# Weights first, two units' mixing shared with ScalarE, and filler transposes in a fused attention and channel-mix kernel

## The chip, the cores and the metric

The kernel runs on one core of a Trainium2 chip, in one launch. The metric is the device time in microseconds (us). A core has four compute engines that matter here: TensorE (PE in the profile: matmuls and transposes), VectorE (DVE), ScalarE (ACT) and GpSimd (POOL). SyncE (SP) issues every DMA. Each engine takes its instructions in the order of the program and waits at the first whose operands are not there.

## The reference

```python
# q, k, v: (8, 8, 576, 64); window 64
scores = q @ k.T / 8, kept where 0 <= i - j < 64
attn = exp(scores - rowmax);  attn /= attn.sum(-1) + 1e-9
x = (attn @ v), heads side by side: (8, 576, 512)
x_prev = x one row later, a zero row first
xk = mu_k * x + (1 - mu_k) * x_prev
xr = mu_r * x + (1 - mu_r) * x_prev
k = relu(xk @ w_k)            # 512 -> 1024
v = (k * k) @ w_v             # 1024 -> 512
out = sigmoid(xr @ w_r) * v
```

All tensors are float32; the three weight matrices come as 8-byte words (float64 bits) and are turned into float32 on the chip.

## The kernel before, in words

**Weights.** The weights are 20 chunks of 128 x 512 words (`chunks`, L169): four of w_r, eight of w_k, eight of w_v, 512 KB each. `load_w` (L173) issues a chunk's DMA, and `decode` (L191) turns it into two float32r parts: one ACT instruction (`sign`), four DVE instructions (`clamp`, `shift`, `top`, `low`: the profile's `wt`, `wp`, `wp`, `wt`), one ACT copy and one POOL subtraction (`ws`). Matmuls take an operand as two parts and make three products of them, so a "piece" of a product is three matmuls.

**Attention.** Blocks of 64 queries are taken in groups `t` of eight, for two heads at once. `burst` (L338) is one PE piece: the scores of group t (tile `s`, 32 small matmuls) and the values of group t-1 (tile `x`, 32). `soften` (L392) does the softmax: per 128 x 128 block a DVE reduction (`least`), an ACT exponential (`exp`), two small DVE instructions (`shares`, tile `rs`), a POOL scaling (`scale`), then four PE transposes into the single PSUM bank `t` (`flip`) and an ACT copy out of it (`keep`, tile `pt`). The result lands in `xT`, channels by tokens, in SBUF.

**Channel mix.** Tokens are taken in 11 units (`UNITS`, L25): 256 tokens, 320, then nine of 448. For each unit `mix` (L467) makes xr and xk in four chunks each: DVE `diff` (tile `d` = x - x_prev), DVE `blend` (d * mu + x_prev), ACT `high`, POOL `low`. `r_units`, `k_units` and `v_units` make the three products of a unit through `product` (L511); their PSUM banks are four of tag `m`, which the decoding also uses.

**Order.** Nothing is issued where it is written. Every step is a `Piece` with an engine, a key (its urgency; 40 keys to a unit, `USTEPS`), a cost in ns, what it needs and what buffers it takes. `play` (L96) runs a small simulation of the engines with those costs, always beginning the ready piece of lowest key, and the order in which pieces begin there is the program order of each engine. `LINK` (50) is the simulated delay from one engine to another. `BEGIN` (L43) has the keys of the groups, `DECODE` (L600) those of the chunks (from -28 to 22), and the transfers are issued in the order of L600 to L621: two pairs' first q and k columns, one chunk, two more pairs, one chunk, the first v columns, mu, three chunks, the rest of q and k, three chunks, the rest of v, the other twelve chunks.

Until the chunks are decoded, PE has only the first groups and unit 0 to work on. From then on its work is unit after unit, with a burst and two flips for every group in between.

Of the kernel before, what the change touches and what calls it, by code (L numbers as in the profile page):

```python
# [17 lines left out]
P = 128  # L18
# [23 lines left out]

BEGIN = (-30, -29, 0, 6, 12, 18, 26, 34, 43, *range(53, 184, 10),  # L43
         196, 210, 223, 236, 250, 263, 277, 286, 295, 304, 312, 322, 332, 342, 352)
LINK = 50

HI_MIN = struct.unpack("<f", struct.pack("<I", 0x38000000))[0]
HI_MAX = struct.unpack("<f", struct.pack("<I", 0x47EFFE00))[0]
# [3 lines left out]
def attn_rwkv_kernel(ctx, tc, qT, kT, v2, mu_k, mu_r, w_k, w_v, w_r, out):  # L52
# [43 lines left out]
    def play():  # L96

        left, free, now, begun = {}, {}, 0, []
        for n, p in enumerate(pieces):
            left.setdefault(p.engine, []).append((p.key, n, p))  # L100
            free[p.engine] = 0
        for e in left:
            left[e].sort(key=lambda x: x[:2])
        users = {id(h): len(h.users) for p in pieces for h in p.takes}
        ends = []
        times = [0]
        while any(left.values()):
            assert times, [(e, [(p.key, p.fn.__name__) for _, _, p in ps[:4]]) for e, ps in left.items()]
            now = heapq.heappop(times)
            while ends and ends[0][0] <= now:  # L110
                _, _, p = heapq.heappop(ends)
                for hold in (*p.takes, *p.uses):
                    users[id(hold)] -= 1
                    if not users[id(hold)]:
                        room[hold.tag] += 1
            for e, ps in left.items():
                if free[e] > now:
                    continue
                for i, (_, n, p) in enumerate(ps):
                    if not all(q.done is not None and q.done + (q.lag if q.engine != e else 0) <= now  # L120
                               for q in p.needs):
                        continue
                    tags = [h.tag for h in p.takes]
                    if any(room[tag] < tags.count(tag) + p.spare for tag in set(tags)):
                        continue
                    del ps[i]
                    for tag in tags:
                        room[tag] -= 1
                    free[e] = now + p.cost
                    p.done = free[e]  # L130
                    begun.append(p)
                    for at in (p.done, p.done + p.lag):
                        heapq.heappush(times, at)
                    heapq.heappush(ends, (p.done + p.lag, n, p))
                    break
        return begun

    def over(n):

# [22 lines left out]

    muk = const.tile([P, NC], F32, name="muk")
    mur = const.tile([P, NC], F32, name="mur")

# [23 lines left out]
    def decode(n, loaded):  # L191
        ws, _, i, c = chunks[n]
        key = DECODE[n]
        word, bits = Hold("tmp"), Hold("m")

        def sign():
            words[n] = tmp.tile([P, WC], F32, name="wt", tag="tmp", bufs=TB)
            sca.activation(words[n], raw[n][:, :, 1].bitcast(F32), AF.Abs)

        def clamp():  # L200
            dve.tensor_scalar(words[n], words[n], HI_MIN, HI_MAX, op0=ALU.max, op1=ALU.min)

        def shift():

            words[n, 0] = ps_m.tile([P, WC], U32, name="wp", tag="m")
            dve.tensor_scalar(words[n, 0], words[n].bitcast(U32), 3, 0x3FFFFFF8,
                              op0=ALU.logical_shift_left, op1=ALU.bitwise_and)

        def top():
            dve.scalar_tensor_tensor(words[n, 0], raw[n][:, :, 1], 0xC0000000, words[n, 0],  # L210
                                     op0=ALU.bitwise_and, op1=ALU.bitwise_or)

        def low():
            dve.scalar_tensor_tensor(words[n].bitcast(U32), raw[n][:, :, 0], 29, words[n, 0],
                                     op0=ALU.logical_shift_right, op1=ALU.bitwise_or)

        def first_part():
            ws[i, c] = const.tile([P, 2, WC], F32R, name="ws", tag="w", bufs=len(chunks))
            sca.copy(ws[i, c][:, 0], words[n])

        def second_part():
            pool.tensor_sub(ws[i, c][:, 1], words[n], ws[i, c][:, 0].bitcast(F32))

        p = Piece("ACT", key, 680, sign, [loaded], takes=[word])
        p = Piece("DVE", key, 420, clamp, [p])
        p = Piece("DVE", key, 700, shift, [p], takes=[bits])
        p = Piece("DVE", key, 700, top, [p])
        p = Piece("DVE", key, 690, low, [p], uses=[bits])
        p0 = Piece("ACT", key, 630, first_part, [p])
        decoded[id(ws), i, c] = p0, Piece("POOL", key, 1280, second_part, [p0], uses=[word])  # L230

# [105 lines left out]

    def burst(t, ts, tv):  # L338

        needs, takes, uses, cost = [], [], [], 200  # L340
        if ts is not None:
            for n, i in (half for halves in groups[ts] for half in halves):
                needs += [arrived[n, i], arrived[n, max(i - 1, 0)], arrived[n, min(max(i, 1), NB - 1)]]
                uses += held[n]
                cost += 54
            takes += [Hold("s"), Hold("s")]
        if tv is not None:
            for n, i, _, _ in order(tv):
                needs.append(arrived[(n, *chunk(i))])
                uses += held["v", n]  # L350
                cost += 61
            needs += chain.pop((tv, "kept"))
            uses += chain.pop((tv, "pt"))
            bank = Hold("x")
# [37 lines left out]
    def soften(t, h, p, bank):  # L392
# [1 line left out]
        key = BEGIN[t]  # L394
        count = len(groups[t])
        rows, sm = Hold("pr"), Hold("sums") if h == 0 else None
        exps = []
        for e in range(count):
            def least(e=e):
                if e == 0:  # L400
# [8 lines left out]
            def exp(e=e):  # L409
# [1 line left out]
                sca.activation(pr[:, e], pr[:, e], AF.Exp, bias=sums[t, h][0][:, e:e + 1], scale=-1.0,  # L411
                               accum_out=sums[t, h][1][:, e:e + 1])

            q = Piece("DVE", key + 0.5, 375, least, [p, exps and softened or None],
                      ([rows] if e == 0 else []), [bank])
            softened = q
            exps.append(Piece("ACT", key + 0.5, 590, exp, [q]))

        def shares():
            rs = sums[t, h][2][:, :count]  # L420
            dve.tensor_scalar_add(rs, sums[t, h][1][:, :count], EPS)
            dve.reciprocal(rs, rs)

        q = Piece("DVE", key + 0.5, 350, shares, exps)
        scaled = []
        for e in range(count):
            def scale(e=e):
                pr = weights[t, h]
                pool.tensor_scalar(pr[:, e], pr[:, e], sums[t, h][2][:, e:e + 1], 1.0, op0=ALU.mult, op1=ALU.mult)

            scaled.append(Piece("POOL", key + 0.5, 400, scale, [q]))

        def flip():
            ps = flipped[t, h] = ps_t.tile([P, G, P], F32, name="t")
# [29 lines left out]
            t += n  # L464
        return found

    def mix(u, mu, xs, hold, c, key):  # L467


        state, scratch = [], Hold("tmp")  # L470
# [1 line left out]
        for b, t0, n in parts(u):  # L472
            ns = b * NP + c

            def diff(o=o, n=n, ns=ns, t0=t0):
                if not xs:
                    xs.append(act.tile([P, 2, NC, TU], F32R, name=hold.tag))
                if o == 0:
                    state.append(tmp.tile([P, TU], F32, name="d", tag="tmp", bufs=TB))
                d = state[0]  # L480
                dve.tensor_sub(d[:, o:o + n], xTs[ns][:, 1 + t0:1 + t0 + n], xTs[ns][:, t0:t0 + n])

            def blend(o=o, n=n, ns=ns, t0=t0):
                d = state[0]
                dve.scalar_tensor_tensor(d[:, o:o + n], d[:, o:o + n], mu[:, c:c + 1], xTs[ns][:, t0:t0 + n],
                                         op0=ALU.mult, op1=ALU.add)

            needs = {got[ns, i] for i in range(max(t0 - 1, 0) // W, (t0 + n) // W)}
            takes = ([scratch] + ([hold] if c == 0 else [])) if o == 0 else []
            p = Piece("DVE", key, over(n), diff, [*needs, p, mixing.get(id(hold))], takes)  # L490
            mixing[id(hold)] = p
            p = Piece("DVE", key, over(n), blend, [p], uses=[held["x", ns]])
            o += n
# [5 lines left out]
            pool.tensor_sub(xs[0][:, 1, c, :o], state[0][:, :o], xs[0][:, 0, c, :o].bitcast(F32))  # L499

        p = Piece("ACT", key, over(o), high, [p])
        return p, Piece("POOL", key, 100 + 2.25 * o, low, [p], uses=[scratch])

    mixing = {}

    def weight(w, a, c, m):

        o = m * P
        return w[c, o // WC][:, a, o % WC:o % WC + P]

    def product(key, w, col, x, made, uses, count, n, spare=0):  # L511


        ps, bank, last = [], Hold("m"), None
        for c in range(count):
            def fn(c=c):
                if c == 0:
                    ps.append(ps_m.tile([P, 512], F32, name="m", tag="m")[:, :n])
                for a, e in ((0, 0), (0, 1), (1, 0)):
# [3 lines left out]
            needs = [last, *made[c], *decoded[id(w), c, col * P // WC]]  # L523
            last = Piece("PE", key + 3 * c / STEP, 3 * (13 + n / 2.4), fn, needs,
                         [bank] if c == 0 else [], uses(c), lag=200, spare=spare if c == 0 else 0)
        return ps, bank, last

    def r_units(key, xr, hold, made, gate, n):
# [23 lines left out]
    def k_units(key, xk, hold, made, k2, n):  # L552
        for f in range(NF):
# [17 lines left out]

            key += 3 * NC / STEP
            p = Piece("ACT", key, over(n), relu, [p], [scratch], [bank])
            p = Piece("POOL", key, 100 + 1.9 * n, square, [p])
            p0 = Piece("ACT", key, over(n), high, [p], [result])
            p1 = Piece("DVE", key, over(n), low, [p0], uses=[scratch])
            k2.append((state, result, (p0, p1)))
# [20 lines left out]


    DECODE = [-28 + 3 * n for n in range(4)] + [-10 + 2 * n for n in range(8)] + [8 + 2 * n for n in range(8)]  # L600
    for n in range(2):
        load_qk(n, 0, 4)
    load_w(1)
    for n in range(2, NP):
        load_qk(n, 0, 4)
    load_w(1)
    for n in range(NP):
        load_v(n, 0, 2, 0, 1)

    def vectors():  # L610
        dma.dma_start(muk, mu_k)
        dma.dma_start(mur, mu_r)

    arrived["mu"] = transfer(vectors, 4096)
    load_w(3)
    for n in range(NP):
        load_qk(n, 4, NB)
    load_w(3)
    for n in range(NP):
        load_v(n, 2, 4, 1, 4)  # L620
    load_w(len(chunks) - len(raw))  # L621
# [13 lines left out]
    for u, nb in enumerate(UNITS):  # L635
# [7 lines left out]
            keys = {"xr": (20, 22, 33, 35), "xk": (25, 27, 29, 31)}  # L643
        else:
            keys = {"xr": [base - 40 + k for k in (33, 35, 37, 39)], "xk": [base - 40 + k for k in (25, 27, 29, 31)]}
        for nm, mu in (("xr", mur), ("xk", muk)):
            hold = Hold(nm)
            xs[nm] = ([], hold, [])
            for c in range(NC):
                xs[nm][2].append(mix(u, mu, xs[nm][0], hold, c, keys[nm][c]))  # L650
        if u == 0:
            r_units(base, *xs["xr"], gate, n)
            k_units(base + 8, *xs["xk"], k2, n)
# [37 lines left out]
```

## Time and profile before

| | us |
|---|---|
| median of 3 runs (lowest, highest) | 689.8 (689.45, 691.6) |
| the profiled execution's own time | 691.39 |
| its span in the profile | 689.6 |
| PE busy in the span | 650.2 |
| DVE busy | 428.1 |
| ACT busy | 366.8 |
| POOL busy | 353.4 |

The span is what the profile covers of the execution; about 1.8 us of the device time lie around it. Busy times are unions of instruction times, and a busy PE need not run at its full clock: the granted clock stands beside it, 1.00 for full and 0.50 for half. In the tables by stretch, each row has the stretch, its length, then each engine's busy us with its count of instructions, the granted clock, the DMA engines' mean share and GB/s. In timelines a row has the start, the length, and the instruction group, with the idle time before it and who ended that in brackets.

### The profile page before, as it was taken

The page shows a single profiled execution, that of the slowest core. Times are in us where ns is not written, and L with a number is a line of the kernel's source. Part 1 is how long each engine was busy: PE and PEld are TensorE (multiplying, and loading weights), DVE is VectorE, ACT ScalarE, POOL GpSimd, SP SyncE. Part 2 cuts the span into 40 slices and gives each one's busy share as a digit, 9 for nine tenths or more (in the row PEclk, how much of TensorE's full clock was granted, in tenths as well). Part 3 has the DMA queues.
Part 4 walks back from the last instruction along what each step waited for, and adds up shares of the span by engine and source line. Part 5 has one row for each costly group of instructions (what it writes and reads, how often), then busy time and mean ns, then how long its engine had stood idle before and what let it go on. Part 6 is the DMA issues. An engine that isn't in the chain of part 4 may idle for free.

```text
span 689.6 us, 14350 instructions
## 1 busy us (share of the span) xinstructions
PE 650.2 (94%) x5232; PEld 583.5 (85%) x5232; DVE 428.1 (62%) x1372; ACT 366.8 (53%) x1111; POOL 353.4 (51%) x503
## 2 busy tenths in 40 slices
PE   5657888999999999999999999999999999999997
PEld 4446787998889888888889788988888889999997
DVE  2998985485487269447926824883595478177241
ACT  5547666656666475466446535736664563242430
POOL 4556776656666455446635543553555464244310
PEclk9756799999999999999999999999999999999999
DMA  8970232233223222322111232123212100001001
GB/s 254 300 316 0 71 127 97 66 114 122 66 67 106 79 66 80 106 82 95 54 52 36 80 106 66 66 66 120 66 46 75 66 2 27 28 1 40 14 1 54
DMA packets 33766, 56.50 MB, mean 82 GB/s; under 512 B 5024, under 2 KB 16800, under 8 KB 33696
## 3 DMA queue, kind: packets, MB, share of 16 engines
q1 hardware_dynamic: 33696, 55.59, 24.3%
q8 instruction: 41, 0.67, 0.4%
q14 instruction: 29, 0.24, 0.1%
HBM read 46.14 MB, written 9.44 MB: 81 GB/s over the span
## 4 chain that ended last, share of the span: by engine, by line
PE 81%; DVE 7%; POOL 4%; DMA 3%; issue 2%; ACT 2%; SPq 1%; POOLq 0%; ACTq 0%
PE m L73 68%; PE x L73 5%; PE s L73 4%; PE t L73 4%; POOL pr L73 2%; DVE wp L73 2%; DVE d L73 2%; DVE wt L73 2%; POOL ws L73 1%; DMA w<-w_k 1%; DMA k<-kT 1%; ACT pr L73 1%; SPq L73 1%; DMA v<-v 1%; DVE r L73 1%
## 5 line engine op out<-in xcount | busy, mean ns | idle before, releaser
L73 PE MATMUL m<-xk,ws 128*128 128x448 f32 (+2 forms) x1056 | 223.9, 365 | 5.1 <-ACT xk L73 1.8
L73 POOL TENSOR_SCALAR pr<-pr,rs 128x128 f32<-128x128 f32 x288 | 139.1, 500 | 146.8 <-DVE rs L73 124.4
L73 PE MATMUL m<-ks,ws 128*128 128x448 f32 (+2 forms) x1056 | 212.8, 357 | 0.0
L73 PEld LDWEIGHTS m<-xk,ws 128*128 128x128 f32 x1056 | 192.0, 195 | 21.1 <-POOL xk L73 2.2
L73 PEld LDWEIGHTS m<-ks,ws 128*128 128x128 f32 x1056 | 187.4, 190 | 13.2
L73 DVE TENSOR_TENSOR ks<-kf,ks 128x448 fp32r<-128x448 f32 (+2 forms) x88 | 62.9, 729 | 125.6 <-ACT ks L73 125.6
L73 PE MATMUL m<-xr,ws 128*128 128x448 f32 (+2 forms) x528 | 114.0, 368 | 13.1 <-ACT r L73 6.2
L73 POOL TENSOR_TENSOR kf<-kf 128x448 f32<-128x448 f32 (+2 forms) x88 | 78.4, 899 | 86.8 <-ACT kf L73 86.7
L73 ACT ACTIVATE pr<-pr,nmax 128x128 f32<-128x128 f32 x288 | 111.8, 393 | 10.8 <-DVE nmax L73 10.8
L73 PEld LDWEIGHTS m<-xr,ws 128*128 128x128 f32 x528 | 96.8, 198 | 22.0 <-ACT r L73 6.5
L73 ACT COPY pt<-t 128x512 f32<-128x512 f32 (+1 forms) x74 | 42.5, 575 | 88.9 <-PE t L73 88.7
L73 DVE TENSOR_TENSOR d<-xT 128x256 f32<-128x256 f32 (+6 forms) x136 | 77.0, 566 | 0.9 <-POOL ws L73 0.6
L73 POOL TENSOR_TENSOR xk<-d,xk 128x448 fp32r<-128x448 f32 (+2 forms) x44 | 56.1, 1284 | 27.3 <-ACT xk L73 24.5
L73 ACT ACTIVATE kf<-m 128x448 f32<-128x448 f32 (+2 forms) x88 | 44.8, 519 | 38.8 <-PE m L73 38.2
L73 POOL TENSOR_TENSOR xr<-d,xr 128x448 fp32r<-128x448 f32 (+2 forms) x44 | 51.6, 1181 | 25.6 <-ACT xr L73 25.5
L73 DVE CUSTOM_DVE_ANT_0 pr<-s,maskNone 128x128 f32<-128x128 f32 x224 | 54.0, 285 | 16.9 <-PE s L73 16.8
L73 ACT CAST ks<-kf 128x448 fp32r<-128x448 f32 (+2 forms) x88 | 46.1, 542 | 30.7 <-POOL kf L73 30.6
L73 PE MATMUL t<-ident,pr 128*128 128x128 f32 x288 | 52.1, 297 | 10.7 <-POOL pr L73 10.4
L73 DVE SCALAR_TENSOR_TENSOR r<-m,r 128x448 f32<-128x448 f32 (+2 forms) x44 | 25.9, 589 | 58.2 <-PE m L73 58.2
L73 PEld LDWEIGHTS t<-ident,pr 128*128 128x128 f32 x288 | 38.6, 148 | 21.0 <-POOL pr L73 16.2
L73 ACT ACTIVATION_READ_ACCUMULATOR pr<-pr,nmax 128x1 f32 x288 | 55.0, 191 | 0.0
L73 PE MATMUL s<-k,q 64*64 64x128 f32 x1152 | 44.2, 291 | 6.0 <-DMA q<-qT 4.5
(41 smaller groups left out, 563.3 us busy)
## 6 DMA issues: line engine op xcount, KB each, us to landing
v<-v SPq DMA_DIRECT2D x56, 256.0 KB, 4.1
k<-kT SPq DMA_DIRECT2D x28, 288.0 KB, 2.8
q<-qT SPq DMA_DIRECT2D x28, 288.0 KB, 3.5
w<-w_k SPq DMA_DIRECT2D x8, 512.0 KB, 7.1
w<-w_v SPq DMA_DIRECT2D x8, 512.0 KB, 10.7
outT<-r SPq DMA_DIRECT2D x12, 224.0 KB, 1.9
w<-w_r SPq DMA_DIRECT2D x4, 512.0 KB, 4.4
outT<-r SPq DMA_DIRECT2D x12, 160.0 KB, 1.8
```

What stands on the lines that cost most here:

```text
L73: return lambda *args, **kw: tc.keep_in_program_order(op(*args, **kw))
```

## The change

Four things change. (1) A weight chunk goes ahead of all transfers, and two of the later ones move up by a place. (2) In units 0 and 1 the first step of the mixing becomes an ACT instruction, (1 - mu) * x_prev, and the DVE step after it mu * x + that; two small DVE instructions make 1 - mu once. (3) Where `play` finds PE free with no ready piece, its clock past 9 us, the bank `t` free and unit 0 not done, it puts in `fill`: two transposes of the identity into bank `t`, which nobody reads. (4) The costs of `play` are other numbers, a step that depends on one of its own engine is ready 30 ns after it, and a product begins only after the product before it has begun.

```diff
+EARLY = 7
-LINK = 50
+LINK = 80
...
-                    if not all(q.done is not None and q.done + (q.lag if q.engine != e else 0) <= now
-                               for q in p.needs):
+                    if not all(q.done is not None and q.done + (q.lag if q.engine != e else 30) <= now for q in p.needs):
...
-                    for at in (p.done, p.done + p.lag):
+                    for at in (p.done, p.done + 30, p.done + p.lag):
                         heapq.heappush(times, at)
                     heapq.heappush(ends, (p.done + p.lag, n, p))
                     break
+                else:
+                    if e == "PE" and room["t"] and now > 9000 and ps and ps[0][0] < USTEPS:
+                        p = Piece("PE", 0, 220, fill, takes=[Hold("t")], lag=0)
+                        users[id(p.takes[0])] = 1
+                        room["t"] -= 1
+                        free[e] = p.done = now + p.cost
+                        begun.append(p)
...
+    def fill():
+        ps = ps_t.tile([P, G, P], F32, name="t")
+        for e in range(2):
+            pe.transpose(ps[:, e, :], ident, ident)
...
-        p = Piece("DVE", key, 420, clamp, [p])
+        p = Piece("DVE", key, 440, clamp, [p])
...
-        needs, takes, uses, cost = [], [], [], 200
+        needs, takes, uses, cost = [], [], [], 400
...
-                cost += 54
+                cost += 109
...
-                cost += 61
+                cost += 122
...
-            q = Piece("DVE", key + 0.5, 375, least, [p, exps and softened or None],
-                      ([rows] if e == 0 else []), [bank])
-            softened = q
-            exps.append(Piece("ACT", key + 0.5, 590, exp, [q]))
+            q = Piece("DVE", key + 0.5, 215 if t < EARLY else 375, least, [p, begin], ([rows] if e == 0 else []), [bank], lag=200)
+            begin = begin or q
+            exps.append(Piece("ACT", key + 0.5, 390 if t < EARLY else 590, exp, [q], lag=280))
...
-            scaled.append(Piece("POOL", key + 0.5, 400, scale, [q]))
+            scaled.append(Piece("POOL", key + 0.5, 365 if t < EARLY else 500, scale, [q]))
...
-                d = state[0]
-                dve.tensor_sub(d[:, o:o + n], xTs[ns][:, 1 + t0:1 + t0 + n], xTs[ns][:, t0:t0 + n])
+                d, x, xp = state[0], xTs[ns][:, 1 + t0:1 + t0 + n], xTs[ns][:, t0:t0 + n]
+                if u < 2:
+                    sca.activation(d[:, o:o + n], xp, AF.Copy, scale=mu1[:, c:c + 1])
+                else:
+                    dve.tensor_sub(d[:, o:o + n], x, xp)
...
+                if u < 2:
+                    dve.scalar_tensor_tensor(d, x, mu[:, c:c + 1], d, op0=ALU.mult, op1=ALU.add)
+                else:
+                    dve.scalar_tensor_tensor(d, d, mu[:, c:c + 1], xp, op0=ALU.mult, op1=ALU.add)
...
-        ps, bank, last = [], Hold("m"), None
+        ps, bank, last = [], Hold("m"), opened[-1]
...
+            if c == 0:
+                opened.append(last)
...
+    load_w(1)
     for n in range(2):
         load_qk(n, 0, 4)
     load_w(1)
     for n in range(2, NP):
         load_qk(n, 0, 4)
+    def rest():
+        dve.tensor_scalar(muk1, muk, -1.0, 1.0, op0=ALU.mult, op1=ALU.add)
+        dve.tensor_scalar(mur1, mur, -1.0, 1.0, op0=ALU.mult, op1=ALU.add)
     load_w(1)
     for n in range(NP):
         load_v(n, 0, 2, 0, 1)
-    arrived["mu"] = transfer(vectors, 4096)
+    arrived["mu"] = Piece("DVE", -25, 300, rest, [transfer(vectors, 4096)])
     load_w(3)
     for n in range(NP):
         load_qk(n, 4, NB)
-    load_w(3)
+    load_w(2)
```

More of the change, by code (lines that the diff above doesn't have):

```diff
@@ L135, in play @@
                     break
-        return begun
+                else:
[5 more added lines that the diff above has]
+                        begun.append(p)
+                        heapq.heappush(times, p.done)
+                        heapq.heappush(ends, (p.done, len(pieces), p))
+        return begun
+    def fill():
+        ps = ps_t.tile([P, G, P], F32, name="t")
+        for e in range(2):
+            pe.transpose(ps[:, e, :], ident, ident)
     def over(n):
@@ L164, in attn_rwkv_kernel @@
     mur = const.tile([P, NC], F32, name="mur")
+    mu1 = const.tile([P, 4, NC], F32, name="mu1")
+    muk1, mur1 = mu1[:, 0], mu1[:, 1]
     wr_s, wk_s, wv_s = {}, {}, {}
@@ L224, in decode @@
         p = Piece("ACT", key, 680, sign, [loaded], takes=[word])
-        p = Piece("DVE", key, 420, clamp, [p])
-        p = Piece("DVE", key, 700, shift, [p], takes=[bits])
-        p = Piece("DVE", key, 700, top, [p])
-        p = Piece("DVE", key, 690, low, [p], uses=[bits])
+        p = Piece("DVE", key, 440, clamp, [p])
+        p = Piece("DVE", key, 725, shift, [p], takes=[bits])
+        p = Piece("DVE", key, 725, top, [p])
+        p = Piece("DVE", key, 725, low, [p], uses=[bits])
         p0 = Piece("ACT", key, 630, first_part, [p])
@@ L396, in soften @@
         rows, sm = Hold("pr"), Hold("sums") if h == 0 else None
-        exps = []
+        exps, begin = [], None
         for e in range(count):
@@ L422, in shares @@
             dve.reciprocal(rs, rs)
-        q = Piece("DVE", key + 0.5, 350, shares, exps)
+        q = Piece("DVE", key + 0.5, 400, shares, exps, lag=200)
         scaled = []
@@ L465, in parts, with mix @@
         return found
-    def mix(u, mu, xs, hold, c, key):
+    def mix(u, mu, mu1, xs, hold, c, key):
         state, scratch = [], Hold("tmp")
@@ L479, in diff @@
                     state.append(tmp.tile([P, TU], F32, name="d", tag="tmp", bufs=TB))
-                d = state[0]
-                dve.tensor_sub(d[:, o:o + n], xTs[ns][:, 1 + t0:1 + t0 + n], xTs[ns][:, t0:t0 + n])
-            def blend(o=o, n=n, ns=ns, t0=t0):
-                d = state[0]
-                dve.scalar_tensor_tensor(d[:, o:o + n], d[:, o:o + n], mu[:, c:c + 1], xTs[ns][:, t0:t0 + n],
-                                         op0=ALU.mult, op1=ALU.add)
+                d, x, xp = state[0], xTs[ns][:, 1 + t0:1 + t0 + n], xTs[ns][:, t0:t0 + n]
[3 more added lines that the diff above has]
+                    dve.tensor_sub(d[:, o:o + n], x, xp)
+            def blend(o=o, n=n, ns=ns, t0=t0):
+                d, x, xp = state[0][:, o:o + n], xTs[ns][:, 1 + t0:1 + t0 + n], xTs[ns][:, t0:t0 + n]
+                if u < 2:
+                    dve.scalar_tensor_tensor(d, x, mu[:, c:c + 1], d, op0=ALU.mult, op1=ALU.add)
+                else:
+                    dve.scalar_tensor_tensor(d, d, mu[:, c:c + 1], xp, op0=ALU.mult, op1=ALU.add)
             needs = {got[ns, i] for i in range(max(t0 - 1, 0) // W, (t0 + n) // W)}
             takes = ([scratch] + ([hold] if c == 0 else [])) if o == 0 else []
-            p = Piece("DVE", key, over(n), diff, [*needs, p, mixing.get(id(hold))], takes)
+            p = Piece("ACT" if u < 2 else "DVE", key, over(n), diff, [*needs, p, mixing.get(id(hold)), arrived["mu"]], takes)
             mixing[id(hold)] = p
@@ L501, in mix @@
         p = Piece("ACT", key, over(o), high, [p])
-        return p, Piece("POOL", key, 100 + 2.25 * o, low, [p], uses=[scratch])
+        return p, Piece("POOL", key, 160 + 2.35 * o, low, [p], uses=[scratch])
     mixing = {}
@@ L509, in weight @@
         return w[c, o // WC][:, a, o % WC:o % WC + P]
+    opened = [None]
     def product(key, w, col, x, made, uses, count, n, spare=0):
-        ps, bank, last = [], Hold("m"), None
+        ps, bank, last = [], Hold("m"), opened[-1]
         for c in range(count):
@@ L573, in k_units @@
             p = Piece("ACT", key, over(n), relu, [p], [scratch], [bank])
-            p = Piece("POOL", key, 100 + 1.9 * n, square, [p])
+            p = Piece("POOL", key, 120 + 1.88 * n, square, [p])
             p0 = Piece("ACT", key, over(n), high, [p], [result])
@@ L605, in attn_rwkv_kernel, with vectors @@
         load_qk(n, 0, 4)
+    def vectors():
+        dma.dma_start(muk, mu_k)
+        dma.dma_start(mur, mu_r)
+    def rest():
+        dve.tensor_scalar(muk1, muk, -1.0, 1.0, op0=ALU.mult, op1=ALU.add)
+        dve.tensor_scalar(mur1, mur, -1.0, 1.0, op0=ALU.mult, op1=ALU.add)
     load_w(1)
@@ L608, in attn_rwkv_kernel @@
         load_v(n, 0, 2, 0, 1)
-    def vectors():
-        dma.dma_start(muk, mu_k)
-        dma.dma_start(mur, mu_r)
-    arrived["mu"] = transfer(vectors, 4096)
+    arrived["mu"] = Piece("DVE", -25, 300, rest, [transfer(vectors, 4096)])
     load_w(3)
@@ L645, in attn_rwkv_kernel @@
             keys = {"xr": [base - 40 + k for k in (33, 35, 37, 39)], "xk": [base - 40 + k for k in (25, 27, 29, 31)]}
-        for nm, mu in (("xr", mur), ("xk", muk)):
+        for nm, mu, mu1 in (("xr", mur, mur1), ("xk", muk, muk1)):
             hold = Hold(nm)
@@ L649, in attn_rwkv_kernel @@
             for c in range(NC):
-                xs[nm][2].append(mix(u, mu, xs[nm][0], hold, c, keys[nm][c]))
+                xs[nm][2].append(mix(u, mu, mu1, xs[nm][0], hold, c, keys[nm][c]))
         if u == 0:
```

## The prediction

> **What bounds the kernel now.** I read the page's totals and PE's row of 40 slices first, then the busy time by stretch.
>
> ```profile
> PE 650.2 (94%) x5232; PEld 583.5 (85%) x5232; DVE 428.1 (62%) x1372; ACT 366.8 (53%) x1111; POOL 353.4 (51%) x503
> ...
> PE   5657888999999999999999999999999999999997
> ```
>
> ```profile
> 0.00:20.00 20.00, 12.12 (x114) 8.58 (x114) 7.60 (x47) 11.15 (x41) 9.89 (x35) 1.00 0.84 268
> 20.00:110.00 90.00, 65.31 (x552) 56.07 (x552) 82.90 (x224) 57.25 (x170) 58.26 (x75) 0.72 0.42 148
> ...
> 120.00:385.00 265.00, 264.54 (x2365) 238.96 (x2364) 166.47 (x593) 155.35 (x491) 148.78 (x217) 1.00 0.25 80
> 385.00:520.00 135.00, 133.14 (x1074) 118.78 (x1073) 81.19 (x286) 72.47 (x226) 69.58 (x98) 1.00 0.22 74
> ```
>
> The 94% of PE hides two stages. From 120 us on PE is full (264.54 of 265 and 133.14 of 135, at clock 1.00): nothing but less PE work, or a stall taken away, shortens that part. Before 110 us PE is busy for 65.31 of 90 at a mean clock of 0.72, which is about 47 us of work at full clock: this head throws away some 43 us of PE, and DVE is the full engine in it (82.90 of 90). The end moves with the time at which the head has let PE do its share. The timeline of DVE says what the head consists of:
>
> ```profile
> 13.74 0.17 DVE L73 TENSOR_SCALAR rs<-sums 128x4 f32<-128x4 f32 x1 [0.79 <-ACT pr L73]
> 16.45 0.17 DVE L73 TENSOR_SCALAR rs<-sums 128x4 f32<-128x4 f32 x1 [2.33 <-ACT pr L73]
> 17.00 0.43 DVE L73 TENSOR_SCALAR wt<-wt 128x512 f32<-128x512 f32 x1 [0.17 <-ACT wt L73]
> ...
> 18.92 0.69 DVE L73 SCALAR_TENSOR_TENSOR wt<-w,wp 128x512 uint32<-128x512 uint32 x1
> ...
> 96.20 0.69 DVE L73 SCALAR_TENSOR_TENSOR wt<-w,wp 128x512 uint32<-128x512 uint32 x1
> ...
> 110.64 0.42 DVE L73 SCALAR_TENSOR_TENSOR r<-m,r 128x256 f32<-128x256 f32 x1
> 114.38 0.29 DVE L73 CUSTOM_DVE_ANT_0 pr<-s,maskNone 128x128 f32<-128x128 f32 x1 [3.32 <-PE s L73]
> ```
>
> The first chunk's decoding starts on DVE at 17.00, the twentieth ends at 96.9, and DVE goes on without a real pause, with the mixing of unit 1, to 111.0; only then does it wait for PE (3.32 us, by a score). So DVE bounds the stretch from 17 to 111, and a us of DVE work that leaves it should bring the saturated stage forward by nearly a us, provided PE and ACT keep up.
>
> **The change, part by part.** The sum goes against the profiled execution, 691.39 us with a span of 689.6; the median of the runs is 1.6 us lower.
>
> *Mixing on ScalarE.*
>
> ```profile
> L73 DVE TENSOR_TENSOR d<-xT 128x320 f32<-128x320 f32 x8 | 4.3, 540 | 0.0
> L73 DVE TENSOR_TENSOR d<-xT 128x256 f32<-128x256 f32 x8 | 3.4, 420 | 0.8 <-POOL ws L73 0.6
> ...
> L73 DVE TENSOR_SCALAR rs<-sums 128x4 f32<-128x4 f32 x14 | 2.4, 172 | 6.8 <-ACT pr L73 6.8
> ...
> L73 ACT CAST xr<-d 128x320 fp32r<-128x320 f32 x4 | 1.8, 459 | 3.0 <-DVE d L73 2.4 <-DVE xT L73 0.6
> ...
> L73 ACT CAST xr<-d 128x256 fp32r<-128x256 f32 x4 | 1.6, 403 | 3.9 <-DVE d L73 3.9
> ```
>
> Sixteen subtractions leave DVE: 3.4 + 4.3 = 7.7 us. The two instructions that make 1 - mu are 128 x 4 like `rs`, 2 x 0.17 = 0.3 us. The blend stays one instruction of the same kind with two tensors, so it costs what it did. Net on DVE: -7.4 us. ACT gets 8 x 0.40 + 8 x 0.46 = 6.9 us, priced by its casts of the same size (the new instruction isn't in the trace). ACT has 57.25 busy in the 90 us, so this fits: with the head some 12 us shorter it would be 64 of 78. If that cover were gone, up to 6.9 us would come back; I take 1.5, for ACT is in order and a step of the mixing queued ahead of an exponential or of a decoding's first step delays what DVE needs next. The new wait on DVE is that of the 1 - mu pair for the mu transfers, with the decodings and reductions queued behind it, and ACT and PE behind those. These transfers are issued near 10.4 (rows below), before DVE's dense work, so I charge nothing; were they late, every us would count in full.
>
> *Weights lead.*
>
> ```profile
> 0.74 0.38 SPq L73 DMA_DIRECT2D k<-kT  x1
> ...
> 2.59 0.43 SPq L73 DMA_DIRECT2D w<-w_r  x1
> ...
> 9.97 0.41 SPq L73 DMA_DIRECT2D muk<-mu_k  x1
> ```
>
> ```profile
> w<-w_r SPq DMA_DIRECT2D x4, 512.0 KB, 4.4
> ```
>
> The first chunk is issued at 2.59 and lands about 4.4 later, at 7, yet DVE begins it at 17: ACT serves exponentials first (DVE's idle time before 17 is ended by `pr`). Issued at 0.74 in the place of k it lands by about 5, when ACT and DVE have nothing, so one decoding (17.00 to 19.61: 2.6 us) leaves the bounded stretch for certain, and the second chunk, up by four transfers, can use DVE's gaps ahead of 17 (the 0.79 and 2.33 above among them). Two decodings are 5.2 us; bounds 2.6 and 7.8. Against it: 512 KB at the 268 GB/s of the first row push q and k, all of them in the queue behind, back by 2.0 us, and with them the first scores; I charge 0.7 for softmax work that slides past 17 us. mu is issued one issue (0.43) later, at 10.4. Net: -4.5.
>
> *Fillers.* First, are the transposes work in the eyes of the clock? In stretches of 2 us the granted clock shows nine changes from here to the full stage; these are the first and the last:
>
> ```profile
> 60.00:62.00 2.00, 2.00 (x24) 0.65 0.00 0
> ...
> 108.00:110.00 2.00, 1.91 (x10) 0.71 0.17 59
> ```
>
> A 0.65 between 0.50 and 1.00 puts the change at 61.4, the 0.71 at 109.2, and all nine lie whole multiples of 3.41 us apart (these two 14), so I cut the head at those multiples. Of each pair below, the second row shows what the first earned:
>
> ```profile
> 47.75:51.16 3.41, 2.76 (x13) 2.46 (x12) 3.31 (x14) 1.91 (x5) 1.32 (x2) 0.50 0.08 32
> 51.16:54.57 3.41, 1.47 (x6) 0.88 (x4) 2.71 (x16) 2.58 (x14) 1.92 (x2) 0.50 0.00 0
> ...
> 64.81:68.23 3.42, 1.70 (x10) 0.93 (x9) 2.15 (x5) 3.42 (x16) 1.68 (x5) 1.00 0.00 0
> 68.23:71.64 3.41, 3.41 (x18) 3.41 (x18) 3.24 (x10) 1.78 (x5) 3.00 (x6) 0.50 0.02 5
> ...
> 105.77:109.19 3.42, 3.33 (x12) 2.94 (x13) 3.28 (x8) 1.60 (x4) 3.42 (x5) 0.50 0.12 38
> 109.19:112.60 3.41, 2.83 (x19) 2.36 (x18) 1.84 (x4) 1.50 (x3) 3.41 (x6) 1.00 0.24 79
> ```
>
> ```profile
> 105.77:109.19 3.42, 1.05 (x4) 0.50 0.12 38
> ```
>
> ```profile
> 16.82 1.12 PE L73 MATMUL t<-ident,pr 128*128 128x128 f32 x4
> ```
>
> ```profile
> 164.29 0.60 PE L73 MATMUL t<-ident,pr 128*128 128x128 f32 x4
> ```
>
> ```profile
> L73 PE MATMUL t<-ident,pr x16: 418/421/477, 10.8 to 19.4; 128*128 128x128 f32 x16
> ```
>
> ```profile
> L73 PE MATMUL t<-ident,pr x288: 270/273/477, 10.8 to 575.9; 128*128 128x128 f32 x144
> ```
>
> A busy 1.70 loses the clock, 2.76 doesn't win it, 3.33 wins it. In that 3.33 lie four transposes (1.05 of modelled time, the one-tile row). In the first 20 us, cold, four take 1.12, of which the last's own 0.42 is latency: (1.12 - 0.42) / 3 = 0.23 us apart; warm, (0.60 - 0.27) / 3 = 0.11. Without them the stretch would hold 3.33 - 4 x 0.23 = 2.4 us, less than the 2.76 that won nothing. So transposes seem to count, and I take it that fillers keep the clock at 1.00 from about 20 us on. (The 1.00 shown before that is not borne out: those sixteen transposes lasted 421 ns, not 273.) The Trainium skill speaks against this: "TensorE: Matmul & The Clock Gate", Part 4 (PE-mode transpose), says that the full clock doesn't engage for transpose mode, which doesn't count as PE-busy in the same way. These rows lean the other way, and no stretch of transposes alone exists here to settle it. By that rule the clock's term below is lost and the time is that of the first rival.
>
> What does the clock buy? Most cold stretches lie beside DVE, which stays the bound. Uncovered is the last: 105.77 to 109.19 has PE at 3.33 of 3.42 at half clock, just ahead of the full stage, 1.7 us; and DVE's shortened stretch needs PE to do the same 47 us in less time, which at 0.72 it would hardly do. I take -1.7; bounds 0 and -5. What do the fillers cost? From 9 us to the end of unit 0 (now about 105, then perhaps 93) the planner has 84 us less some 50 of PE work, so roughly 35 us to fill, 160 fillers of 2 x 0.11 = 0.22 us, which is also the cost that the planner uses. In PE's idle time they are free; one that stands ahead of work that is ready costs 0.22. And a filler's bank must have been emptied by ACT's copy, so PE can stall at it with products queued behind. I take 7 in the way, +1.5; bounds 0 and 12 (a third of them).
>
> *The planner's costs.* They change the order everywhere. In the full stage the matmuls are the same and go back to back from whichever product they come, so the interleaving that the 30 ns cause there costs nothing; it can only move stalls. By the row from 385 to 520 us above, PE idles there for 1.9 us in all, and for 0.5 from 120 to 385. The chain of waits shows the larger place:
>
> ```profile
> 389.71 0.62 DVE r L73
> ...
> 392.40 3.34 POOL pr L73 x3
> ...
> 395.79 0.33 PE t L73
> ...
> 402.31 1.03 PE s L73 x32
> 403.34 1.08 PE x L73 x32
> ```
>
> Transposes wait for a scaling on POOL that DVE released late; the chain leaves PE for 6.1 us (389.7 to 395.8), but PE has other products for most of them, so this is worth its idle time and not its length. A burst is priced at 2248 now instead of 1120, and takes 1.03 + 1.08 us in these rows; so the order should run closer to the chip, and I take -0.5; bounds -2.4 (all idle time gone) and +6 (a wait as long as this one, uncovered).
>
> Sum: -7.4 + 1.5 - 4.5 - 1.7 + 1.5 - 0.5 = -11.1, so 691.4 - 11.1 = 680.3 against its own time, 678.7 against the median. I say 679.
>
> **The rivals.** *The fillers run cold, and it gets slower.* If transposes don't count, a PE stream with fillers between products hardly ever wins the clock: 160 fillers at 0.46 instead of 0.22 add 38 us, just where the planner had filled the gaps, and the products beside them run at half rate too. It decides once the fillers' stretch is at 0.50 for about a third of its length. Price: 38 less the 11.1, so 718 us at least. For it: no stretch of transposes alone; against: the 2.4 against 2.76 above.
>
> *ACT takes DVE's place.* The head then holds 64 us of ACT work in 78, in order, and reductions, decodings and blends on DVE all pass through an ACT step. Most of the 7.4 would be given back (5.9 beyond the 1.5 charged) and the weights' 4.5 and the rest stay: 686.2 by its own time, 684.6 by the median. For it: DVE's own waits in the rows above are on ACT (`pr`). Against: ACT idles for 33 of its 90 us.
>
> *The fillers stand in the way.* The planner's idle time isn't the chip's. With a third of the fillers ahead of ready work, 12 us instead of 1.5, the gain is eaten: 690.8.
>
> *The full stage stalls more.* The order is new for 570 us. Two uncovered waits of 6.1 us like the one shown, 12.2 instead of -0.5, bring 693.0.
>
> **How the numbers follow.** Forecast 0.56; its own range is 671 to 684: from 679 down by 2.6 for a third decoding, 1.9 for the idle time left and 3.3 for the rest of the clock's bound, and up by the terms of the fillers and of ACT, each 1.5, growing to 4. ACT 0.18; fillers in the way 0.10; full stage 0.08; cold fillers 0.08. Under 0.3%, 2 us, a measurement of this kernel tells nothing from no change (its three runs spread over 2.15). Faster: 0.56 + 0.16 + 0.03 + 0.02 = 0.77; slower: 0.01 + 0.05 + 0.04 + 0.08 = 0.18; the same: the 0.05 left. The range 669 to 689 takes in the forecast and the ACT case, with some 2 us on either side for the runs' spread, and leaves out most of the other three.
>
> **What would show it.** Right: first decoding on DVE at about 5 us, last ending near 86; granted clock 1.00 from 20 to 110; ACT near 64 us in the head with few DVE waits on it; PE full from about 98; under 3 us of PE idle past 120. Wrong: 0.50 in stretches full of transposes; DVE idle between 20 and 95 behind ACT; PE waiting for ACT's copies at a filler; new PE gaps past 120 us.

## The result, and the profile after

The changed kernel takes 709.26 us (median of 4 runs, 708.71 to 709.85) against 690.46 for the kernel before in the same comparison: a ratio of 1.0272, 95% interval 1.0251 to 1.0293. It is 18.8 us slower, where 11 us faster was forecast, and outside the range. The profiled execution took 708.71 us, with a span of 706.9.

The totals and the slices of the page of after:

```profile
PE 684.9 (97%) x5536; PEld 595.5 (84%) x5536; DVE 426.3 (60%) x1358; ACT 372.6 (53%) x1127; POOL 347.5 (49%) x503
...
PE   5899999999999999999999999999999999999997
...
DVE  5790786477378349636863933792497289167241
...
PEclk9999999999999999999999999999999999999999
```

PE is fuller by 34.7 us and has 304 instructions more, and its clock is shown at 90% or more in all slices: the fillers fill the gaps and hold the clock, as they were expected to. DVE is not the full engine of the head any more: its fourth slice, 53 to 71 us, is a 0. Busy time by stretch, after:

```profile
0.00:20.00 20.00, 12.40 (x132) 7.57 (x132) 10.50 (x53) 12.13 (x43) 11.13 (x34) 1.00 0.84 259
20.00:40.00 20.00, 18.07 (x160) 12.28 (x160) 16.75 (x36) 14.66 (x38) 11.89 (x15) 1.00 0.99 353
40.00:60.00 20.00, 17.91 (x94) 9.37 (x91) 13.32 (x35) 7.67 (x20) 10.06 (x13) 1.00 0.34 139
60.00:80.00 20.00, 18.42 (x161) 12.38 (x162) 9.01 (x34) 8.15 (x29) 4.04 (x5) 1.00 0.00 1
```

```profile
120.00:600.00 480.00, 476.91 (x4103) 428.17 (x4102) 304.10 (x1045) 274.56 (x864) 256.75 (x376) 1.00 0.22 74
```

For before the same stretch reads

```profile
120.00:600.00 480.00, 477.68 (x4028) 430.27 (x4027) 294.10 (x1017) 266.47 (x829) 255.27 (x365) 1.00 0.22 72
```

so the full stage has lost 0.8 us (3.1 idle instead of 2.3). The loss is in the head: from 40 to 80 us PE is busy for 18 of each 20 us, and the other three engines for 4 to 13. PE's timeline of after, where DVE has its hole:

```profile
39.41 0.61 PE L74 MATMUL m<-xr,ws 128*128 128x256 f32 x3
39.85 14.78 PE L74 MATMUL t<-ident 128*128 128x128 f32 x60
54.39 0.60 PE L74 MATMUL m<-xr,ws 128*128 128x256 f32 x3
...
56.12 0.60 PE L74 MATMUL m<-xr,ws 128*128 128x256 f32 x3
56.56 10.81 PE L74 MATMUL t<-ident 128*128 128x128 f32 x44
67.52 0.63 PE L74 MATMUL t<-ident,pr 128*128 128x128 f32 x4
```

```profile
56.60:67.40 10.80, 9.55 (x46) 4.33 (x43) 0.00 (x0) 0.00 (x0) 0.00 (x0) 1.00 0.00 0
```

```profile
68.19 0.59 ACT L74 COPY pt<-t 128x512 f32<-128x512 f32 x1 [17.63 <-PE t L74]
```

```profile
69.37 0.69 DVE L74 TENSOR_SCALAR wp<-wt 128x512 uint32<-128x512 uint32 x1 [15.94 <-ACT r L74]
```

Thirty fillers (sixty transposes) take 14.78 us and twenty-two take 10.81: 0.49 us each, not 0.22. While the second run of them lasts, DVE, ACT and POOL do nothing at all: ACT is in its queue at the copy of a flip that stands behind the fillers (17.63 us), DVE waits for ACT (15.94), and the decoding stands still. The chain of waits of after shows what a filler consists of, and the list of who waits for whom shows why:

```profile
56.96 0.04 issue
57.00 0.45 PE t L74 x2
57.45 0.04 issue
57.50 0.45 PE t L74 x2
```

```profile
  PE t L74: 35.2, 118
```

(That row counts, over all instructions that use the identity, the idle time that an earlier PE instruction on tile `t` ended: 35.2 us, 118 times. By the same view it is the weight loads, PEld in the profile, that wait.) A filler takes a new tile from a pool with one buffer, so it begins only when the filler before it has ended, with the latency of its last transpose: 0.45 us and 0.04 for the issue.

### The profile page after: what moved, and what is told of

Read it like the earlier page. It is cut to its first block, busy times and chain, and to the rows that moved or that the text cites. A ratio compares the mean times of both kernels' runs of the same rounds, so it can differ in the third digit from the quotient of the medians.

```text
span 706.9 us, 14968 instructions
## 1 busy us (share of the span) xinstructions
PE 684.9 (97%) x5536; PEld 595.5 (84%) x5536; DVE 426.3 (60%) x1358; ACT 372.6 (53%) x1127; POOL 347.5 (49%) x503
## 4 chain that ended last, share of the span: by engine, by line
PE 88%; DVE 5%; POOL 3%; issue 2%; DMA 1%; ACT 1%; POOLq 0%; ACTq 0%
PE m L74 65%; PE t L74 12%; PE s L74 5%; PE x L74 5%; POOL pr L74 2%; DVE d L74 1%; DVE r L74 1%; DVE pr L74 1%; DMA w<-w_r 1%; DVE ks L74 1%; DVE th L74 0%; DMA k<-kT 0%; POOL xr L74 0%; DVE wp L74 0%; DVE rs L74 0%
## 5 line engine op out<-in xcount | busy, mean ns | idle before, releaser
L74 PE MATMUL m<-xk,ws 128*128 128x448 f32 (+2 forms) x1056 | 220.8, 357 | 0.0
L74 PE MATMUL m<-ks,ws 128*128 128x448 f32 (+2 forms) x1056 | 219.6, 357 | 0.0
L74 PEld LDWEIGHTS m<-xk,ws 128*128 128x128 f32 x1056 | 185.9, 188 | 14.0
L74 POOL TENSOR_SCALAR pr<-pr,rs 128x128 f32<-128x128 f32 x288 | 133.4, 481 | 111.4 <-DVE rs L74 97.9
L74 PE MATMUL m<-xr,ws 128*128 128x448 f32 (+2 forms) x528 | 112.2, 357 | 0.0
L74 PEld LDWEIGHTS m<-xr,ws 128*128 128x128 f32 x528 | 93.4, 188 | 6.8
L74 PE MATMUL t<-ident 128*128 128x128 f32 x304 | 65.6, 298 | 7.5 <-ACT pt L74 0.7
L74 DVE TENSOR_TENSOR d<-xT 128x448 f32<-128x448 f32 (+6 forms) x120 | 72.1, 604 | 0.2
L74 PEld LDWEIGHTS t<-ident 128*128 128x128 f32 x304 | 32.2, 142 | 36.8 <-PE t L74 35.2
L74 DVE CUSTOM_DVE_ANT_0 pr<-s,maskNone 128x128 f32<-128x128 f32 x224 | 54.0, 285 | 12.4 <-PE s L74 12.1
L74 PE MATMUL t<-ident,pr 128*128 128x128 f32 x288 | 45.5, 275 | 5.0 <-POOL pr L74 1.7
```

The costliest lines, as they stand in the source:

```text
L74: return lambda *args, **kw: tc.keep_in_program_order(op(*args, **kw))
```

## The experiments

**Is it the fillers, and is it their length?** The next kernels tell three theories apart: *the length* (fillers cost about twice their price, since each waits for the one before), *the place* (the planner's gaps are not the chip's, so fillers of any length are in the way) and *the order* (the new costs are bad by themselves).

*No fillers*, all else as changed:

```diff
-                    if e == "PE" and room["t"] and now > 9000 and ps and ps[0][0] < USTEPS:
+                    if False and room["t"] and now > 9000 and ps and ps[0][0] < USTEPS:
```

> The changed kernel without any filler; all else as changed. First theory (a filler waits for the filler before it, so 152 of them take 0.49 us each instead of the 0.22 that the planner gives them, and hold up PE for some 40 us more than its gaps): with them gone the 17 us of loss vanish and the other parts show, 680 to 685 us, with the clock at 0.50 in places again. Second theory (the planner's gaps are not the chip's gaps, so fillers of any length stand in the way): the same here. Third theory (the new order itself is worse, by the 30 ns rule and the other costs): 700 us or more.

Measured 678.84 us, ratio to before 0.9823 (0.9808 to 0.9837), 1.2 us below the range that was expected. The rest of the change gains 12.1 us; the order falls as a cause of the loss.

*The same fillers, neighbours in one tile*, so that none waits for the one before:

```diff
-        ps = ps_t.tile([P, G, P], F32, name="t")
+        if not open_t:
+            open_t.append(ps_t.tile([P, G, P], F32, name="t"))
         for e in range(2):
-            pe.transpose(ps[:, e, :], ident, ident)
+            pe.transpose(open_t[0][:, e, :], ident, ident)
...
+            open_t.clear()
             ps = flipped[t, h] = ps_t.tile([P, G, P], F32, name="t")
```

> The changed kernel with the same 304 filler transposes at the same places, but fillers that follow one another write into one and the same tile, so none waits for the end of the one before; only the first after a kept transpose takes a new tile. First theory: a pair takes 0.22 us as planned, the stretches of 60 transposes that last 14.8 us shrink to 6.6, 678 to 686 us with the clock at 1.00. Second theory: the places are wrong whatever the length; part of the loss goes, 692 us or more. Third theory: 700 us or more.

Measured 679.85 us, ratio 0.9841 (0.9825 to 0.9856). Its PE timeline and its stretches:

```profile
32.38 6.71 PE L74 MATMUL t<-ident 128*128 128x128 f32 x60
```

```profile
20.00:90.00 70.00, 68.38 (x771) 63.43 (x772) 68.14 (x186) 54.38 (x158) 50.75 (x66) 1.00 0.53 185
```

The same 304 transposes at the same places of PE's order; sixty of them now take 6.71 us, 0.22 a pair, and DVE is full again (68.14 of 70). The waits between fillers are all that differs, and they are worth 709.26 - 679.85 = 29.4 us; the 35.2 us of idle time in the row above are of that size, and that row is missing in this kernel. The place falls.

*The right price*, 490 ns in the planner, which then places 64 fillers:

```diff
-                        p = Piece("PE", 0, 220, fill, takes=[Hold("t")], lag=0)
+                        p = Piece("PE", 0, 490, fill, takes=[Hold("t")], lag=0)
```

> The changed kernel with the filler's price in the planner at 490 ns, what a pair takes on the chip when it follows another, instead of 220; the planner then places 64 fillers instead of 152. First theory: plan and chip agree, 678 to 686 us, the clock mostly at 1.00. Second theory: 692 us or more. Third theory: 700 us or more.

Measured 678.71 us, ratio 0.9823 (0.9801 to 0.9845). Fillers as long as the changed kernel's do no harm where the plan knows their length. There are fewer of them, but the plan gives them about the same time in all: 64 x 0.49 = 31 us, against 152 x 0.22 = 33.

*Four transposes per filler*, in one tile, at the old price of 220 ns:

```diff
-        for e in range(2):
+        for e in range(4):
```

> The kernel with one tile for neighbouring fillers, but four transposes in each filler instead of two: about 0.44 us each without any wait, still priced at 220 ns. If it is the length beyond the price that costs, whatever makes it, this repeats the loss: 700 to 712 us. If the wait between fillers costs in some way of its own (the semaphore, an emptied pipeline), it stays near the kernel with one tile: 680 to 688 us.

Measured 709.1 us, ratio 1.027 (1.0253 to 1.0286): the changed kernel's time again, without its wait. Its run of fillers in the same place:

```profile
39.63 13.26 PE L74 MATMUL t<-ident 128*128 128x128 f32 x120
```

So it is the length beyond the price that costs, whatever makes it: 0.44 us a filler by more work, 0.49 by a wait, and the same loss.

*The fillers alone on the kernel before*, with no other part of the change:

> The kernel before with nothing but the fillers added, at 220 ns; its planner places 200 of them. First and second theory: 200 x 0.49 = 98 us of PE time where the kernel before lost some 43 us of it in waiting and at half clock: 715 to 740 us, with the clock at 1.00. Third theory (the fillers are cheap and the order is the loss): 690 us or less.

Measured 741.62 us, ratio 1.0705 (1.0659 to 1.0752), and a last decoding that ends at 142 us instead of 97. That is 1.6 us above the range of the first two theories. Both the length and the place expected such a loss; it excludes only cheap fillers.

**What are the other parts worth?** Each alone on the kernel before, as in the diff of the change.

> The kernel before with only the mixing of units 0 and 1 shared with ScalarE (and the two small instructions for 1 - mu). Theory of the sum: 7.4 us leave DVE, which is the full engine of the head, and ACT has room: 683 to 686 us. Rival (ACT takes DVE's place or the old order spoils it): 688 us or more.

Measured 684.22 us, ratio 0.9913 (0.9896 to 0.993): -6.7 us.

> The kernel before with only the order of the transfers changed. Theory of the sum: one or two decodings move into the time before 17 us, 685 to 688 us. Rival (the old costs let ACT serve the exponentials first all the same, and the scores come 2 us later): 690 to 693 us.

Measured 691.53 us, ratio 1.0011 (1.0001 to 1.0021): nothing. Its first 20 us (those of before stand in the prediction):

```profile
0.00:20.00 20.00, 10.88 (x110) 8.10 (x111) 7.60 (x47) 11.16 (x41) 10.88 (x36) 1.00 0.81 265
```

DVE does 7.60 us there, as before: a decoding went in at 5.1 us, and as much of the rest slid out. The last `rs` pair of this stretch starts at 17.27 us instead of 16.45, and then DVE waits for ACT (`xT`) until 19.76, where before it began to decode at 17.00.

> The kernel before with only the planner's costs, the 30 ns and the order of products of the changed kernel; no fillers, old mixing, old transfers. Theory of the sum: -0.5 us, 688 to 692. Rival (the new order is what gains, since the head of the kernel without fillers had its last decoding 21 us earlier, more than the work that left DVE explains): 684 us or less.

Measured 682.48 us, ratio 0.9887 (0.9872 to 0.9902): -8.4 us from the planner's costs and rules alone; the sum's -0.5 falls. Its first 20 us:

```profile
0.00:20.00 20.00, 11.30 (x114) 7.85 (x114) 12.29 (x56) 12.85 (x44) 11.67 (x37) 0.91 0.81 260
```

DVE does 12.29 us instead of 7.60. It also pauses less after that; from 20 to 90 us, before and with the new costs:

```profile
20.00:90.00 70.00, 48.16 (x403) 40.74 (x402) 63.86 (x172) 45.21 (x130) 42.58 (x52) 0.68 0.49 170
```

```profile
20.00:90.00 70.00, 46.75 (x447) 39.87 (x451) 67.41 (x179) 47.98 (x141) 47.76 (x62) 0.80 0.51 180
```

The next two split the costs: softmax steps alone (the hunk of `soften`, which has prices, delays and one dependency), and all but these.

> The kernel before with only the softmax steps' prices and delays of the changed kernel. First theory (the planner had priced an exponential at 590 ns where it takes 390, so it saw ACT as full in the first 17 us and let the decoding wait; the right price moves a decoding or two up): 684 to 687 us, first decoding near 9 to 12 us. Second theory (the gain of the costs alone comes from the others: bursts, the delay of 80, the 30 ns, the order of products): 689 us or more.

Measured 685.03 us, ratio 0.993 (0.9904 to 0.9955): -5.8 us.

```profile
L74 DVE TENSOR_SCALAR wt<-wt x20: 397/420/1321, 11.9 to 89.0; 128x512 f32<-128x512 f32 x20
L74 DVE SCALAR_TENSOR_TENSOR wt<-w,wp x20: 657/686/690, 14.5 to 92.2; 128x512 uint32<-128x512 uint32 x20
```

(First and last start of a step.) The first decoding begins on DVE at 11.9 us instead of 17.0 and the last ends at 92.9 instead of 96.9, as its first theory had it.

> The kernel before with all the costs of the changed kernel except the softmax steps'. First theory: little, 687 to 692 us. Second theory: it holds most of the 8.4 us that all the costs gave, 682 to 685 us.

Measured 691.89 us (689.4 to 695.69 over ten runs), ratio 1.0034 (1.0012 to 1.0057): nothing gained alone. In the profiled run, the fastest of the ten (689.4 us), the head did gain: its first decoding begins at 8.6 us and its last ends at 90.9. But the full stage lost:

```profile
120.00:600.00 480.00, 473.87 (x3920) 424.28 (x3919) 296.81 (x996) 262.13 (x812) 251.11 (x355) 1.00 0.22 70
```

PE idles for 6.1 us there instead of 2.3. With the softmax prices the same costs come to -8.4, where the two apart come to -4.6; why the softmax prices give back what the full stage lost was not taken apart further.

*Costs and mixing*, without fillers and with the old order of the transfers:

> The changed kernel without fillers and without the new order of the transfers: the costs and the shared mixing together. First theory (the weights' lead is worth nothing, since with the new costs the decoding moves ahead of 17 us anyway): within 1.5 us of the kernel without fillers, 677 to 680 us. Second theory (the lead has its worth once ACT lets the first decoding in): 681 us or more.

Measured 677.03 us, ratio 0.9813 (0.9785 to 0.9842): the fastest median here, ahead of both kernels, and not to be told from the kernel without fillers (0.9808 to 0.9837). The lead of the weights has no worth under the new costs either.

*Costs and mixing with fillers at 490 ns:*

> The costs and the mixing, old transfers, and fillers at 490 ns in the planner. First theory (a filler that fits its gap is free and buys nothing, since DVE and not the clock bounds the head): within 1.5 us of the kernel with costs and mixing alone, 675.5 to 678.5 us, though the clock is higher in the head. Second theory (the higher clock is worth the 1.7 us or more of the prediction): 675 us or less.

Measured 678.88 us, ratio 0.9827 (0.9802 to 0.9851). From 20 to 90 us, with those fillers and without any:

```profile
20.00:90.00 70.00, 61.77 (x629) 48.02 (x627) 67.03 (x190) 57.71 (x166) 53.31 (x70) 1.00 0.54 189
```

```profile
20.00:90.00 70.00, 51.57 (x521) 43.72 (x522) 67.03 (x193) 56.46 (x168) 50.33 (x66) 0.85 0.52 186
```

A clock of 1.00 instead of 0.85, the same 67.03 us of DVE, and no gain. The time is a little above the range of the first theory (1.85 us from the kernel without these fillers, not within 1.5); the second theory falls.

One landmark goes with these times: the end of the last decoding on DVE, from the last start of `wt<-w,wp` and its 0.69 us.

| kernel | last decoding ends, us | median, us |
|---|---|---|
| before | 96.9 | 690.5 to 691.0 |
| weights first only | 97.7 | 691.5 |
| softmax prices only | 92.9 | 685.0 |
| costs only | 90.4 | 682.5 |
| other costs only | 90.9 | 691.9 |
| mixing only | 88.5 | 684.2 |
| no fillers | 85.7 | 678.8 |
| right price | 83.5 | 678.7 |
| one tile | 86.2 | 679.9 |
| costs and mixing | 83.0 | 677.0 |
| the same, fillers at 490 | 84.6 | 678.9 |
| after | 115.6 | 709.3 |
| four per filler | 114.7 | 709.1 |
| fillers on before | 142.3 | 741.6 |

From before to after the landmark moves by 18.7 us and the time by 18.8; to fillers on before by 45.4 and 51; on the side of the gains the two agree within 2 us, to either side. The exception is the kernel with the other costs only, with its loss in the full stage.

## Why the prediction was wrong

**The step that failed** is the price of a filler: "160 fillers of 2 x 0.11 = 0.22 us, which is also the cost that the planner uses". The count was nearly right (152), and 0.22 is right for two transposes in a row. But a filler in a run takes 0.49, because its tile comes from a pool of one buffer and waits for the filler before it. The prediction named the one wait of that bank that an engine other than PE ends (ACT's copy) and not the one on PE itself. As the code has a new tile in every filler, and the rows of warm transposes gave the latency of 0.27 us, most of it was there to be read: 0.11 + 0.27 = 0.38. What makes up the other 0.11 was not taken apart. The term was +1.5 with a bound of +12; the fillers, with all that they do to the clock, measured 709.26 - 678.84 = 30.4 us.

**Its rival** "the fillers stand in the way" had the mechanism's place right (fillers ahead of ready work, on an engine that takes its instructions in order) and the size wrong: 690.8. It took some of the fillers at 0.22 for misplaced; with one tile the same places cost 1.0 us (679.85 against 678.84), within the intervals, so what cost was the length of each filler in a run.

**The bound** held: DVE's work decides the head. In the changed kernel without fillers, with one tile and with the right price DVE is busy for 67 to 68 of 70 us from 20 to 90, and the time follows its last decoding. But "without a real pause" read too much into the timeline: before, DVE was busy for 63.86 of these 70 us, with the new costs alone for 67.41.

**Mixing on ScalarE**: -5.9 in the sum, -6.7 measured. ACT did not take DVE's place. The new instruction costs more than the casts by which it was priced, in the kernel without fillers 506 and 563 ns:

```profile
L74 ACT ACTIVATE d<-xT,mu 128x320 f32<-128x320 f32 x8 | 4.3, 563 | 0.4 <-POOL xr L74 0.4
L74 ACT ACTIVATE d<-xT,mu 128x256 f32<-128x256 f32 x8 | 4.1, 506 | 0.0
```

That is 8.4 us on ACT and not 6.9, still under cover. The Trainium skill, "ScalarE: Activation LUTs", What ACT_TABLE_LOAD costs, states that each operand taken by pointer adds about 93 ns; 506 - 403 and 563 - 459 agree within some 10 ns, as the scale is such an operand and the casts have none. No run here changes that operand alone.

**Weights lead**: -4.5 in the sum, nothing measured, with the old costs and with the new. The argument that a decoding in idle time leaves the bounded stretch left out what comes behind it: the softmax steps slid by some 0.8 us, and DVE stood still just after them, until 19.76 us. An early first decoding is not enough; the time follows the last one, which ended 0.8 us later.

**The planner's costs**: -0.5 in the sum, -8.4 measured. I looked for their worth in the long stage, where there was no idle time to win, and not in the head, where the order decides when DVE begins to decode. The first step of a decoding on ACT (`wt`) starts at 16.3 us before, at 10.1 with the softmax prices alone and at 6.8 with the other costs alone. So the old price of an exponential, 590 ns where the chip takes 391, is not the only number that held the decoding back, and no run changes it alone.

**The clock**: -1.7 in the sum, no gain measured: kernels with fillers of the length that the plan gives them (679.85 and 678.71 against 678.84 without, 678.88 against 677.03) differ from those without in the clock and not, beyond their intervals, in time. No run has the higher clock without the fillers that bring it, so a small gain that they themselves eat is not excluded. That transposes count for the clock is borne out as far as they keep it. That the last cold stretch was uncovered does not hold for the changed kernel: without fillers its clock is 1.00 from 80 us on, and its last decoding ends at 85.7.

So the sum of the other parts, -5.9 - 4.5 - 0.5 = -10.9, is close to the -12.1 of the kernel without fillers, but by luck: the errors of two terms (weights and costs) cancel for the most part. Nor do the parts simply add: mixing and costs give -6.7 and -8.4 apart and -13.8 together.

**The other rivals.** The fillers did not run cold in the changed kernel: 1.00 from 20 us on. The full stage stalled more by 0.8 us, not by 12; only the other costs alone came to 3.8 more.

## What to carry to other kernels

Work that fills an engine's gaps must be priced with what it waits for and not only with what it does: in an order fixed ahead of time every filler that is longer than its price pushes all that stands behind it on that engine, and through it every engine that waits. A new tile from a pool of one buffer is a wait for the instruction before, even on one engine: here 0.49 us for two transposes instead of 0.22. Before filling gaps to raise a clock, ask whether the clocked engine sets the end: here the costs and rules by which an order was planned were worth 8 us, and the higher clock brought no gain that the runs could tell.

## What the runs showed of the hardware that was not expected

Transposes alone hold the full clock. In after, sixty of them fill 39.85 to 54.4 us, and PE's busy time there is 12.37 us of 14 by the model, with the clock at 1.00. Over all fillers of this kernel the median transpose takes 273 ns, as the warm ones of before do, and not 421:

```profile
40.00:54.00 14.00, 12.37 (x59) 5.63 (x56) 13.32 (x35) 7.67 (x20) 10.06 (x13) 1.00 0.49 199
```

The Trainium skill, "TensorE: Matmul & The Clock Gate", Part 4 (PE-mode transpose), says that the full clock doesn't engage for transpose mode; here, in float32, the measurement decides against it as far as keeping the clock goes. Whether transposes alone can win it back from 0.50 no run isolates. In the kernel with fillers on before, runs of fillers that waited for each other did not win it early on (four pairs in 2.93 us, 0.73 each: cold, for the four kept transposes just behind them take 1.08 us, though the clock is shown as 1.00 there), and after a dense burst of scores and values sixteen pairs took 0.50 each:

```profile
25.06 2.93 PE L73 MATMUL t<-ident 128*128 128x128 f32 x8 [0.74 <-ACT pt L73]
...
31.98 1.07 PE L73 MATMUL x<-pt,vs 128*64 128x64 f32 x16
32.98 8.01 PE L73 MATMUL t<-ident 128*128 128x128 f32 x32
```
